# First weight blocks on a second DMA queue, and idle matmuls on a built-in constant

## The chip, the cores and the metric

The kernel runs on one core of one Trainium2 chip. The metric is the device time of one execution in microseconds: 135.92 us, the median of three runs (135.65 to 135.99). A core has five engines that run side by side, each with its own list of instructions: PE (TensorE, matrix products; its weight loads are listed as PEld), DVE (VectorE), ACT (ScalarE), POOL (GpSimd) and SP (SyncE, which here only issues DMAs). ACT and POOL can issue DMAs as well. An instruction that needs another engine's or a transfer's result waits on a semaphore, and everything behind it on its engine waits too.

## What is computed

Two branches over the same x of 2048 rows and 512 columns in bf16, mixed by a gate:

```
g = sigmoid((x * gate_w).sum(-1))
a = irfft2(rfft2(x) * (w_r + 1j * w_i))            # 2048 x 257 spectrum
h = x @ w1 + b1;  act = h * tanh(softplus(h));  b = act @ w2    # F = 1792
out = g * a + (1 - g) * b
```

The branch b is two dense layers with a Mish activation between them; the branch a is a Fourier filter, done as matrix products with small constant matrices and two exchanges through DRAM.

## The kernel before, in words

x is handled as 16 tiles of 128 rows, in 4 chunks of 4 tiles; w1's 1792 columns as 14 blocks of 128 (ft), and its 512 rows as 4 parts of 128 (dt). For a chunk, each x tile is transposed on PE (L516) with a permutation matrix as the weights, evicted from PSUM by DVE or ACT (L529 for the first chunk, L446 and L447 after), and then multiplied with the blocks of w1 (layer 1, L575); ACT applies Mish with the bias b1 while it evicts (L560). The second layer is L903. The steps of the filter branch (L609 to L612, L630, L745, L798, L828, L846) lie between them, and the layers fill PE where the filter branch waits.

The order of each engine's instructions is not written by hand. Every piece of work is a task with an engine, a planned duration, what it reads and writes, and a priority. `schedule` (L215) goes through the ready tasks, takes the one that can begin first by its own estimates (of those within 0.1 us the one with the highest priority), and so fixes a list for each engine. DMAs have a planned transfer time from their bytes and a rate `bw`; in the kernel before, all transfers of SP and ACT are planned as one line, one behind another (`dq_free`, L236 and L288 to L291). DMAs of one engine are issued in the order of the source. A planned duration affects only the order that is built, not the work.

The head is written apart. x's first chunk comes in two loads, `ld_x0(0)` for tiles 0 and 2 and `ld_x0(1)` for tiles 1 and 3 (L464). w1's first four blocks come in four loads, one for each of the 4 row parts (`ld_w1d`, L467), 128 KB each in rows of 1024 bytes. SP issues, in this order: x0(0), w1d0, x0(1), w1d1, w1d2, w1d3, w1's blocks 4 to 8 (512 KB), FD (a constant of the filter branch), x's second chunk (512 KB), w1's blocks 8 to 14, and the rest. ACT issues b1 alone (L474); POOL waits for w1's last load before it issues its own loads of w_r, w_i and w2. As soon as a pair of tiles and a row part of w1 are there, PE multiplies them: `early` for tiles 0 and 2, one row part at a time, `late` for tiles 1 and 3, one block at a time (both L590). b1 is transposed by a small product (L519) and evicted by ACT (`ev_small`, L521).

Until x arrives PE runs idle matmuls (`warm`, L502 to L505), whose results nobody reads. Their operand is a tile of zeros, `zt`, which DVE sets first (L500); they have 128 columns of weights and stream 256 columns. They are fillers: the planner puts one in wherever nothing better can begin on PE, and drops the rest when the first `early` task is planned (L239 to L243, L597). 14 of them are in the profile. The "table" task (L501) is an activation on one column, there so that ACT loads its function table early; it reads `zt` as well.

Of the kernel before, what the change touches and what calls it, by code (L numbers as in the profile page):

```python
# [7 lines left out]
BF = mybir.dt.bfloat16  # L8
F32 = mybir.dt.float32
AF = mybir.ActivationFunctionType  # L10
# [156 lines left out]
class _Graph:  # L167
# [47 lines left out]
    def schedule(self):  # L215
        tasks = self.tasks
        for t in tasks:
            t.succ = []
            t.start = -1.0
        for t in tasks:  # L220
            for d in t.deps:
                d.succ.append(t)
        for t in reversed(tasks):
            m = 0.0
            for s_ in t.succ:
                if s_.bl > m:
                    m = s_.bl
            t.bl = t.dur + t.lat + m
        nleft = {id(t): len(t.deps) for t in tasks}
        ready = [t for t in tasks if not t.deps]  # L230
        free = {e: 0.0 for e in self.ENGS}
        order = {e: [] for e in self.ENGS}
        nsched = 0
        EPS = SCH['eps']
        SYNC_LAT = SCH['sync']
        dq_free = 0.0  # L236
        dq2_free = 0.0
        while nsched < len(tasks):
            if self.filled is not None and self.filled.start >= 0:  # L239
                nsched += sum(t.filler for t in ready)  # L240
                ready = [t for t in ready if not t.filler]
                self.filled = None
                continue  # L243
            first = {}
            for t in ready:
                if t.isdma and t.idx < first.get(t.eng, 1 << 30):
                    first[t.eng] = t.idx
            best = None
            best_est = None
            ests = []  # L250
            for t in ready:
                if t.isdma and t.idx != first[t.eng]:
                    continue
                if t.opts is None:
                    est = free[t.eng]
                    for d in t.deps:
                        dd = d.done + SYNC_LAT + t.slack if d.eng != t.eng else d.start + d.dur if d.eng == "pe" else d.done
                        if dd > est:
                            est = dd
                else:  # L260
                    bo = None
                    for (oe, od, of) in t.opts:
                        e_ = free[oe]
                        for d in t.deps:
                            dd = d.done + (0.0 if d.eng == oe else SYNC_LAT)
                            if dd > e_:
                                e_ = dd
                        sc = e_ + od + (OPT_BIAS.get(oe, 0.0) if (self.win_first is not None and self.win_first.start >= 0 and self.win_last.start < 0) else 0.0)
                        if bo is None or sc < bo[0] - 1e-9:
                            bo = (sc, e_, oe, od, of)  # L270
                    est = bo[1]
                    t.eng, t.dur, t.fn = bo[2], bo[3], bo[4]
                ests.append((est, t))
                if best_est is None or est < best_est:
                    best_est = est
            best = None
            for est, t in ests:
                if est <= best_est + EPS:
                    if best is None:
                        best = (est, t)  # L280
                    elif (t.prio, t.bl, -t.idx) > (best[1].prio, best[1].bl, -best[1].idx):
                        best = (est, t)
            est, t = best
            ready.remove(t)
            t.start = est
            free[t.eng] = est + t.dur
            if t.isdma:
                if t.eng in ("sp", "act"):  # L288
                    xs = max(est + t.dur + 1.0, dq_free)
                    dq_free = xs + t.xfer  # L290
                    t.done = dq_free + 0.6 + 0.4 * (est > 12.0)  # L291
                else:
                    xs = max(est + t.dur + 1.2, dq2_free)
                    dq2_free = xs + t.xfer * 1.5
                    t.done = dq2_free + 1.0
            else:
                t.done = est + t.dur + t.lat + LAT[t.eng]
            order[t.eng].append(t)
            nsched += 1
            for s_ in t.succ:  # L300
                nleft[id(s_)] -= 1
                if nleft[id(s_)] == 0:
                    ready.append(s_)
        self.order = order
        self.makespan = max(t.done for t in tasks)
        return order
# [9 lines left out]
def _build(nc, A_x, A_w_r, A_w_i, B_x, B_w1, B_b1, B_w2, gate_w, out):  # L316
    cs = _build_consts()
    d_FD = nc.inline_tensor(_bf16_bits(cs["FD"]), name="c_fd").bitcast(BF)
# [7 lines left out]
    G = _Graph()  # L326
    es = ExitStack()
    with es:
        def sb(name, shape, dt):
            return es.enter_context(nc.sbuf_tensor(name, shape, dt))  # L330

        xo = sb("xo", [128, NT, 512], BF)
# [4 lines left out]
        act = sb("act", [128, 3, NFT, 512], BF)  # L337
        w1_sb = sb("w1_sb", [128, 4, F], BF)
        w2_sb = sb("w2_sb", [128, NFT, 512], BF)
        FDs = sb("FDs", [128, 768], BF)  # L340
# [6 lines left out]
        Ybuf = sb("Ybuf", [128, 32 * KR], BF)  # L347
        junk = sb("junk", [128, 512], BF)
        gwb = sb("gwb", [128, 512], BF)
        zt = sb("zt", [128, 256], BF)  # L350
        braw = sb("braw", [14, 128], BF)
        b1f = sb("b1f", [128, NFT], F32)
        gdot = sb("gdot", [128, NT], F32)
# [10 lines left out]
        xs = sb("xs", [128, 2, 2, 16], F32)  # L364
        rs = sb("rs", [128, 2, 16], F32)
        q1 = sb("q1", [128, 2, 2, 16], F32)
# [25 lines left out]
        ps = es.enter_context(nc.psum_tensor("ps", [128, 8, 512], F32))  # L392
        psb = ps.bitcast(BF)

        xv = A_x[0].rearrange("(s p b) d -> p s b d", s=2, b=8)
# [16 lines left out]
        def dma(name, dst, src, reads=(), writes=(), nbytes=0, deps=(), is_out=False, prio=None, queue="sp", bw=300e3):  # L412
            dur = 1.0 if queue == "pool" else 0.5

            def fn(e, _dst=dst, _src=src):
                return e.dma_start(_dst, _src)

            t = G.add(name, queue, dur, fn, reads=reads, writes=writes, lat=2.0 + nbytes / bw, deps=deps, prio=prio)
            t.xfer = nbytes / bw
            t.isdma = True  # L420
            if is_out:
                t.sem = out_sem
                n_out_dma[0] += 1
                t.semval = 16 * n_out_dma[0]
            else:
                t.sem = new_sem("d_" + name)
                t.semval = 16
            return t
# [30 lines left out]

        def ld_x(c, s0, s1):  # L460
            dma(f"ld_x{c}{s0}", xo[:, 4 * c + 2 * s0:4 * c + 2 * s1, :].rearrange("p (s b) d -> p s b d", b=2), xv[:, s0:s1, 2 * c:2 * c + 2, :],
                writes=[("x", t) for t in range(4 * c + 2 * s0, 4 * c + 2 * s1)], nbytes=128 * 2048 * (s1 - s0), bw=330e3 if c == 1 else 380e3)

        def ld_x0(b):  # L464
            dma(f"ld_x0{b}", xo[:, b:4:2, :], xv[:, :, b, :], writes=[("x", b), ("x", 2 + b)], nbytes=128 * 2048, bw=(218e3, 350e3)[b])

        def ld_w1d(dt_):  # L467
            dma(f"ld_w1d{dt_}", w1_sb[:, dt_, 0:512], w1v[:, dt_, 0:512], writes=[("w1d", dt_)], nbytes=128 * 1024, bw=350e3)

        def ld_w1(lo, hi):  # L470
            return dma(f"ld_w1_{lo}", w1_sb[:, :, 128 * lo:128 * hi], w1v[:, :, 128 * lo:128 * hi],
                       writes=[("w1", f) for f in range(lo, hi)], nbytes=512 * 256 * (hi - lo), bw=220e3 if lo == 4 else 380e3)

        dma("ld_b1", braw[:, :], B_b1.rearrange("(ft p) -> ft p", p=128), writes=["braw"], nbytes=3584, queue="act", prio=100.0)  # L474
        ld_x0(0)
# [1 line left out]
        ld_x0(1)  # L477
        for dt_ in range(1, 4):
            ld_w1d(dt_)
        ld_w1(4, 8)  # L480
        dma("ld_fd", FDs[:], d_FD[:], writes=["FD"], nbytes=128 * 1536, bw=262e3)
        ld_x(1, 0, 2)
        t_w1 = ld_w1(8, 14)
        dma("ld_m1", m1g1[:, 0:2048], d_M1.rearrange("p b h c m -> p (b h c m)"), writes=["m1"], nbytes=128 * 4096)
# [12 lines left out]
                writes=[("w2", h)], nbytes=128 * 7 * 1024, queue="pool", deps=[t_w1])  # L497


        G.add("zero", "dve", 0.15, lambda e: e.memset(zt[:, :], 0.0), writes=["zt"], prio=99.0)  # L500
        G.add("table", "act", 1.5, lambda e: e.activation(q1[:, 0, 0, 0:1], zt[:, 0:1], AF.Mish), reads=["zt"], prio=99.0)  # L501
        for i in range(NWARM):  # L502
            n_ = 256 if i < 15 else 128
            G.add(f"warm{i}", "pe", n_ / 1200, lambda e, n_=n_: e.matmul(ps[:, 6, 0:n_], zt[:, 0:128], zt[:, 0:n_], start=True, stop=True),  # L504
               reads=["zt"], prio=1.0).filler = True  # L505


        SP0 = PR['sp0']
        s1_tasks = []
        t_r1w = []  # L510
        def f_tr(e, ts, dts, at):
# [6 lines left out]

        pe("tr_small", 0.1, lambda e: e.transpose(psb[:, 0, 0:14], braw[0:14, :], id14[:, :]),  # L519
           reads=["braw", "id14"], writes=[("bank", 0)], prio=SP0 + 4.0)  # L520
        G.add("ev_small", "act", 0.25, lambda e: e.activation(b1f[:, :], psb[:, 0, 0:14], AF.Copy), reads=[("bank", 0)], writes=["b1f"], prio=SP0 + 1.05)  # L521
        for b in range(2):
            for dt_ in range(4):
                bk = (dt_ + 1) % 4
# [507 lines left out]
```

## Time and profile before

| | |
|---|---|
| median of three runs | 135.92 us (135.65 to 135.99) |
| the profiled execution: its time | 135.63 us |
| its span, first to last instruction | 133.9 us |
| PE, DVE, ACT, POOL busy | 96%, 66%, 59%, 20% |
| PE's share of the chain that ended last | 90% |
| loads: issue and time to landing | x0(0) 0.80 + 2.7; w1d0 1.31 + 3.4; x0(1) 1.81 + 3.6; w1 4 to 8 3.74 + 5.8; x's second chunk 4.76 + 7.0 us |

Times in the profile are from the first instruction, in us; a row of the timeline has the start, the length, the engine, the line, the operation with what it writes and reads, and how many instructions are merged in it. A matmul's own duration, from its start to its modelled end, is longer than the distance to the next one, since they are pipelined; the distance tells the rate. In a table by stage, each row has the stage, its length, PE's busy time and instructions, the clock that PE was granted, the busy share of the 16 DMA engines and GB/s.

### The profile page before, as it was taken

Reading aid. Unit: us, or ns where it says so; the run is one execution under the profiler, and the core shown is the slowest. Engines: PE = TensorE matmul, PEld = TensorE weight load, DVE = VectorE, ACT = ScalarE, POOL = GpSimd, SP = SyncE. Lnnn points to the kernel's source line nnn. Section 1 sums busy time; section 2 is a strip of 40 time slices with the busy share of each in tenths; the row PEclk is TensorE's granted clock in tenths of the full one; section 3 lists DMA queues with packets and bytes.
Section 4 is the critical chain, followed back from the end, with each engine's and each line's share of the span. In section 5 each row is a group of like instructions: output and inputs, shape, how many; then the busy total and the mean of one; then the engine's idle time right before and its main releaser. Section 6 shows DMA issues by size and latency. Waiting matters only on the chain.

```text
span 133.9 us, 2695 instructions
## 1 busy us (share of the span) xinstructions
PE 128.9 (96%) x1030; PEld 69.5 (52%) x1047; DVE 88.9 (66%) x213; ACT 79.6 (59%) x130; POOL 27.4 (20%) x56
## 2 busy tenths in 40 slices
PE   6999999999999999999999999999999999999992
PEld 4885655655544443443443443443445877755452
DVE  0286298989689982963893893794001699999422
ACT  4258798899988786605256657434333789792000
POOL 2000793014000009583440440440000000000000
PEclk9999999999999999999999999999999999999999
DMA  3899999999262399450600600600649700305321
GB/s 114 238 294 367 397 284 299 288 366 344 62 157 58 99 293 334 98 220 0 157 5 0 157 2 0 156 6 0 157 150 277 204 2 0 130 32 215 113 102 42
DMA packets 18937, 20.82 MB, mean 155 GB/s; under 512 B 1196, under 2 KB 16172, under 8 KB 18540
## 3 DMA queue, kind: packets, MB, share of 16 engines
q1 hardware_dynamic: 17888, 16.67, 41.1%
q0 software_dynamic: 864, 3.94, 9.4%
q8 instruction: 8, 0.13, 0.4%
q10 hardware_dynamic: 172, 0.04, 0.1%
q14 instruction: 5, 0.04, 0.1%
HBM read 14.35 MB, written 6.29 MB: 154 GB/s over the span
## 4 chain that ended last, share of the span: by engine, by line
PE 90%; ACT 6%; issue 1%; DVE 0%
PE ps L903 34%; PE ps L575 31%; PE ps L846 5%; ACT act L560 3%; PE ps L828 3%; ACT Ybuf L447 3%; PE ps L504 2%; PE ps L516 2%; PE ps L886 2%; PE ps L612 2%; PE ps L590 2%; PE ps L798 2%; PE ps L745 2%; PE ps L630 1%; PE ps L609 1%
## 5 line engine op out<-in xcount | busy, mean ns | idle before, releaser
L575 PE MATMUL ps<-xT,w_sb 128*128 128x512 bf16 x199 | 48.1, 379 | 0.8 <-issue 0.2
L903 PE MATMUL ps<-w_sb,act 128*128 128x512 bf16 x202 | 46.9, 379 | 0.6 <-issue 0.3
L560 ACT ACTIVATE act<-ps,b1f 128x512 bf16<-128x512 f32 x56 | 37.8, 692 | 12.8 <-PE ps L575 10.9
L903 PEld LDWEIGHTS ps<-w_sb,act 128*128 128x128 bf16 x210 | 20.2, 98 | 23.2 <-issue 1.2
L575 PEld LDWEIGHTS ps<-xT,w_sb 128*128 128x128 bf16 x208 | 19.4, 98 | 22.3 <-issue 2.1
L756 DVE TENSOR_TENSOR misc<-ps,WT 128x512 f32<-128x512 f32 x32 | 19.8, 681 | 5.9 <-PE ps L745 5.9
L858 ACT ACTIVATE xo<-ps,omg 128x512 bf16<-128x512 f32 x12 | 8.3, 690 | 19.5 <-PE ps L903 18.9
L762 POOL TENSOR_TENSOR misc<-misc 128x255 bf16<-128x255 f32 x17 | 12.1, 732 | 18.4 <-DVE misc L756 18.4
L446 DVE CAST Ybuf<-ps 128x512 bf16<-128x512 f32 (+1 forms) x9 | 8.2, 926 | 9.1 <-PE ps L798 7.3
L850 ACT ACTIVATE misc<-ps,gcol 128x512 f32<-128x512 f32 x16 | 10.7, 692 | 2.5 <-PE ps L846 2.4
L853 DVE TENSOR_TENSOR Tg<-misc 128x256 bf16<-128x256 f32 x32 | 11.7, 419 | 0.6 <-ACT misc L850 0.5
L446 DVE CAST misc<-ps 128x512 bf16<-128x512 f32 x7 | 4.8, 687 | 10.5 <-PE ps L828 10.5
L447 ACT ACTIVATE Ybuf<-ps 128x512 bf16<-128x512 f32 (+1 forms) x15 | 9.9, 714 | 2.9 <-PE ps L798 2.8
L649 DVE SCALAR_TENSOR_TENSOR junk<-xo,gwb 128x512 bf16<-128x512 bf16 x16 | 11.0, 690 | 0.7
L846 PE MATMUL ps<-GDs,misc 128*128 128x256 bf16 x64 | 9.3, 273 | 0.0
L447 ACT ACTIVATE Abuf<-ps 128x512 bf16<-128x512 f32 x13 | 7.7, 604 | 0.0
L446 DVE COPY xT<-ps 128x512 bf16<-128x512 bf16 x10 | 4.2, 422 | 4.6 <-PE ps L516 4.5
L516 PEld LDWEIGHTS ps<-pid,xo 128*128 128x128 bf16 x64 | 5.6, 111 | 3.1 <-DVE xT L446 0.4
L846 PEld LDWEIGHTS ps<-GDs,misc 128*128 128x128 bf16 x64 | 6.0, 98 | 2.1
L516 PE MATMUL ps<-pid,xo 128*128 128x128 bf16 x64 | 6.8, 243 | 0.0
L781 POOL TENSOR_TENSOR gexp<-gbase,gdot 128x16 f32<-128x16 f32 x1 | 2.9, 2943 | 18.5 <-DVE junk L649 18.5
L612 PE MATMUL ps<-FDs,Tg 128*128 128x256 bf16 x32 | 6.0, 273 | 0.0
(85 smaller groups left out, 112.8 us busy)
## 6 DMA issues: line engine op xcount, KB each, us to landing
scr<-Ybuf SPq DMA_DIRECT2D x16, 256.0 KB, 3.9
Abuf<-scr SPq DMA_DIRECT2D x4, 512.0 KB, 5.8
Abuf<-scr SPq DMA_DIRECT2D x8, 256.0 KB, 4.9
w_sb<-in_B_w_dram POOLq DMA_DIRECT2D x2, 896.0 KB, 14.2
out_dram<-xo SPq DMA_DIRECT2D x7, 256.0 KB, 2.1
xo<-in_A_x_dram SPq DMA_DIRECT2D x3, 512.0 KB, 9.8
WT<-in_A_w_r_dram POOLq DMA_DIRECT2D x4, 257.0 KB, 9.1
WT<-in_A_w_i_dram POOLq DMA_DIRECT2D x4, 257.0 KB, 10.8
```

The costliest lines, as they stand in the source:

```text
L446: G.add_multi(name, [("dve", dve_dur(n, rate=rate), lambda e: e.tensor_copy(out=dst, in_=src)), ("act", act_dur(n), lambda e: e.activation ...
L447: ("act", act_dur(n), lambda e: e.activation(dst, src, AF.Copy))],
L516: ins = e.transpose(psb[:, bank, 128 * col:128 * col + 128], xo[:, t, 128 * dt_:128 * (dt_ + 1)], perm[:, :])
L560: lambda e: e.activation(act[:, c % 3, ft, :].rearrange("p (t a b) -> p t a b", t=4, b=4), ps[:, bank, :].rearrange("p (t b a) -> p t a b" ...
L575: ins = e.matmul(ps[:, bank, :], w1_sb[:, dt_, 128 * ft:128 * (ft + 1)], xT[:, dt_, 4 * c:4 * c + 4, :], start=(dt_ == 0), stop=(dt_ == 3))
L649: lambda e, t=t: e.scalar_tensor_tensor(out=junk[:, :], in0=xo[:, t, :], scalar=1.0, in1=gwb[:, :], op0=ALU.mult, op1=ALU.mult, accum_out= ...
L756: lambda e, Pb=Pb, Wu=Wu, h=h, uu=uu, pb=pb: e.tensor_tensor(out=Pb[:, pb, :].rearrange("p (c j m) -> p c j m", c=2, j=2), in0=ps[:, 2 * h ...
L762: fz = (lambda e, c=c, Pb=Pb, op=op, pb=pb, h=h, uu=uu, zb=zb: e.tensor_tensor(out=Zb[:, zb, h, c, uu, 1:256], in0=Pb[:, pb, 1:256], in1=P ...
L846: ins = e.matmul(ps[:, yk, 256 * (j // 2):256 * (j // 2) + 256], TT[:, ts_, j // 2, s1, j % 2, :], GDs[:, j, :], start=(j % 2 == 0), stop= ...
L850: G.add(f"geo_{t}", "act", act_dur(512, True), lambda e: e.activation(gEO[:, gb, :], ps[:, yk, :], AF.Copy, scale=gcol[:, t:t + 1]), reads ...
L853: fg = (lambda e, i=i, op=op: e.tensor_tensor(out=ga[:, t, 256 * i:256 * i + 256], in0=gEO[:, gb, 0:256], in1=gEO[:, gb, 256:512], op=op))
L903: ins = e.matmul(ps[:, bank, :], act[:, hb, ft, 128 * tl:128 * (tl + 1)], w2_sb[:, ft, :], start=(ft == 0), stop=(ft == NFT - 1))
```

## The change

It has four parts. The loads `ld_w1d` of w1's first four blocks are issued by ACT, two ahead of the table task and two behind it by their priorities, and the planner keeps a line of its own for each of the two issuers. On SP the load of blocks 4 to 8 is split into 4 to 6 ahead of FD and 6 to 8 behind it, so that its rows have 512 bytes. The idle matmuls and the table task read a built-in constant of 1.0 that the start-up code sets on every core before any engine begins (it is a float32 column, read with a step of zero), in place of `zt`, which goes together with its memset; the idle matmuls have 32 columns of weights and stream 128 columns (the first eight) or 64. The eviction of the transposed b1 goes from ACT to DVE. Besides, planned rates and durations are changed, on which the order depends.

```diff
-        dq_free = 0.0
+        dq_free = {"sp": 0.0, "act": 0.0}
...
-                    xs = max(est + t.dur + 1.0, dq_free)
-                    dq_free = xs + t.xfer
-                    t.done = dq_free + 0.6 + 0.4 * (est > 12.0)
+                    xs = max(est + t.dur + 1.0, dq_free[t.eng])
+                    dq_free[t.eng] = xs + t.xfer
+                    t.done = xs + t.xfer + 0.6 + 0.4 * (est > 12.0)
...
-        zt = sb("zt", [128, 256], BF)
...
-                writes=[("x", t) for t in range(4 * c + 2 * s0, 4 * c + 2 * s1)], nbytes=128 * 2048 * (s1 - s0), bw=330e3 if c == 1 else 380e3)
+                writes=[("x", t) for t in range(4 * c + 2 * s0, 4 * c + 2 * s1)], nbytes=128 * 2048 * (s1 - s0), bw=210e3 if c == 1 else 380e3)
...
-            dma(f"ld_x0{b}", xo[:, b:4:2, :], xv[:, :, b, :], writes=[("x", b), ("x", 2 + b)], nbytes=128 * 2048, bw=(218e3, 350e3)[b])
+            dma(f"ld_x0{b}", xo[:, b:4:2, :], xv[:, :, b, :], writes=[("x", b), ("x", 2 + b)], nbytes=128 * 2048, bw=(330e3, 200e3)[b])
...
-            dma(f"ld_w1d{dt_}", w1_sb[:, dt_, 0:512], w1v[:, dt_, 0:512], writes=[("w1d", dt_)], nbytes=128 * 1024, bw=350e3)
+            dma(f"ld_w1d{dt_}", w1_sb[:, dt_, 0:512], w1v[:, dt_, 0:512], writes=[("w1d", dt_)], nbytes=128 * 1024, bw=(125e3, 150e3, 262e3, 262e3)[dt_],
+                queue="act", prio=99.8 - 0.5 * (dt_ > 1))
...
-                       writes=[("w1", f) for f in range(lo, hi)], nbytes=512 * 256 * (hi - lo), bw=220e3 if lo == 4 else 380e3)
+                       writes=[("w1", f) for f in range(lo, hi)], nbytes=512 * 256 * (hi - lo), bw={4: 160e3, 6: 291e3}.get(lo, 380e3))
...
-        ld_w1(4, 8)
-        dma("ld_fd", FDs[:], d_FD[:], writes=["FD"], nbytes=128 * 1536, bw=262e3)
+        ld_w1(4, 6)
+        dma("ld_fd", FDs[:], d_FD[:], writes=["FD"], nbytes=128 * 1536, bw=200e3)
+        ld_w1(6, 8)
...
-        G.add("zero", "dve", 0.15, lambda e: e.memset(zt[:, :], 0.0), writes=["zt"], prio=99.0)
-        G.add("table", "act", 1.5, lambda e: e.activation(q1[:, 0, 0, 0:1], zt[:, 0:1], AF.Mish), reads=["zt"], prio=99.0)
+        ones = nc.const_aps.tensor(1.0, (128, 256))
+        G.add("table", "act", 1.5, lambda e: e.activation(q1[:, 0, 0, 0:1], ones[:, 0:1], AF.Mish), prio=99.5)
         for i in range(NWARM):
-            n_ = 256 if i < 15 else 128
-            G.add(f"warm{i}", "pe", n_ / 1200, lambda e, n_=n_: e.matmul(ps[:, 6, 0:n_], zt[:, 0:128], zt[:, 0:n_], start=True, stop=True),
-               reads=["zt"], prio=1.0).filler = True
+            n_ = 128 if i < 8 else 64
+            G.add(f"warm{i}", "pe", n_ / 600, lambda e, n_=n_: e.matmul(ps[0:32, 6, 0:n_], ones[:, 0:32], ones[:, 0:n_], start=True, stop=True),
+                  prio=1.0).filler = True
...
-        G.add("ev_small", "act", 0.25, lambda e: e.activation(b1f[:, :], psb[:, 0, 0:14], AF.Copy), reads=[("bank", 0)], writes=["b1f"], prio=SP0 + 1.05)
+        G.add("ev_small", "dve", 0.15, lambda e: e.tensor_copy(out=b1f[:, :], in_=psb[:, 0, 0:14]), reads=[("bank", 0)], writes=["b1f"], prio=SP0 + 1.05)
...

```

## The prediction

> **What bounds the kernel now.** I read the page's busy times, then PE's own waits, then the table by stage, then PE's timeline of the head and the landings of the first loads.
>
> ```profile
> PE 128.9 (96%) x1030; PEld 69.5 (52%) x1047; DVE 88.9 (66%) x213; ACT 79.6 (59%) x130; POOL 27.4 (20%) x56
> ...
> PE 90%; ACT 6%; issue 1%; DVE 0%
> ...
> PE ps L504 <- DVE zt L500: 1.1, 1, 1.1
> PE ps L903 <- issue: 0.3, 2, 0.2
> PE ps L575 <- issue: 0.2, 1, 0.2
> PE ps L575 <- ACT act L560: 0.2, 1, 0.2
> ...
> 1.11:4.31 3.20, 3.19 (x16) 1.00 0.65 202
> 4.31:7.20 2.89, 2.89 (x23) 1.00 0.86 234
> 7.20:10.10 2.90, 2.90 (x28) 1.00 0.92 297
> 10.10:40.00 29.90, 29.25 (x322) 1.00 0.91 286
> ...
> 1.11 2.10 PE L504 MATMUL ps<-zt 128*128 128x256 bf16 x9 [1.11 <-DVE zt L500]
> 3.15 0.19 PE L519 MATMUL ps<-pid,braw 14*128 14x14 bf16 x1
> 3.27 1.25 PE L504 MATMUL ps<-zt 128*128 128x256 bf16 x5
> 4.31 1.06 PE L516 MATMUL ps<-pid,xo 128*128 128x128 bf16 x8
> 5.16 1.06 PE L590 MATMUL ps<-xT,w_sb 128*128 128x256 bf16 x4
> 6.01 1.06 PE L516 MATMUL ps<-pid,xo 128*128 128x128 bf16 x8
> 6.87 3.40 PE L590 MATMUL ps<-xT,w_sb 128*128 128x256 bf16 x28
> ...
> L590 PE MATMUL ps<-xT,w_sb x6: 344/421/421, 5.2 to 7.1; 128*128 128x256 bf16 x6
> ...
> L590 PE MATMUL ps<-xT,w_sb x28: 272/273/421, 6.9 to 10.0; 128*128 128x256 bf16 x28
> ```
>
> PE is the bound from 4.31 us on: after its first instruction it waits for nothing longer than 0.2 us, and between 10.1 and 131.5 us it idles only about 1.5 us. A shift of the head is therefore passed on to the end almost whole, and nothing later than the head is touched by the diff except through the planner's order.
>
> In the head two things count. First, PE runs at half rate until about 7.1 us: four L590 matmuls take 6.01 - 5.16 = 0.85 us, 0.213 each for 256 columns, and their rows read 421 ns; later rows read 273 ns and some 27 fill the 2.90 us from 7.20 on, about 0.108 each. (The clock column says 1.00 in these first stages; the matmul rows contradict it.) Second, real work starts at 4.31 although the first x load, issued at 0.80, lands 2.7 us later, at 3.50. The gap is five more idle matmuls of L504, planned ahead and not to be interrupted.
>
> **The change, part by part.**
>
> *Start of the idle matmuls.* They no longer wait for DVE's memset (0.17 us, begun at 0.89). SP and ACT leave the start barrier at 0.80; PE can too. They start 0.31 us earlier. The "table" activation loses the same wait, which its DMA issue (ACT is busy to 1.47) covered anyway.
>
> *How long they last.* The planner fills PE until the first transposes can go. Worked by hand with its changed entries, that is eight of 128 columns and ten of 64, some 1664 columns, against 14 of 256 before. What a column costs no row shows, for the constant is float32. The low end is the bf16 row: 0.213/256 = 0.83 ns, 1.39 us in all, and then x's landing binds. The high end is matmuls that do not overlap at all: the L516 rows at half clock are 314 ns for 128 columns, so some 260 for 64, and 8 x 0.314 + 10 x 0.26 = 5.1 us. I take twice the bf16 row, 2.77 us, since the element has four bytes instead of two; between the ends it is the nearer to neither, and the entry in the diff (columns/600) says the same. With 0.25 us around the small transpose (3.03 to 3.27 now), the idle block ends at 0.80 + 2.77 + 0.25 = 3.82. Weight loads (151 ns for 128 columns at half clock, here 32) lie under the matmuls; uncovered they would add at most 18 x 0.151 = 2.7 us, which lies inside the high end.
>
> *First x.* It is first on SP's queue as before and shares the DMA engines only from about 2.6 us (w1's first block, issued by ACT at 1.47, plus the 1.15 us that x needs from issue to first packet). It lands between 3.50 as now and, at half the rate for the last 70 KB, 3.8. With 0.2 us from weight load to matmul the transposes start between 3.8 and 4.05. I take 3.82: 0.49 us earlier than 4.31. This is work at half rate, worth 0.24 us at full rate.
>
> *The clock step.* It came 6.0 us after the first idle matmul. If it follows the start of activity it comes 0.31 us earlier, worth 0.155 us; if it stays where it was, nothing. [...]
>
> *w1 on ACT.* SP loses four issues of 0.45 us, and gains one for the split of block 4 to 8; x's fourth issue onward goes out 1.5 us sooner. ACT gains four issues: after b1 (0.80 to 1.47) two, to 2.4; then table load and activation (1.28 + 0.20), to 3.9; then two more, to 4.8. Its first eviction is due at about 4.6 instead of 4.98 and would wait up to 0.2 us; who waits is the second set of transposes, due at 5.5, so this is covered. If the sequencer issues past the table load they go out at 2.5 and nothing waits. w1's blocks landed at 4.7, 6.0, 6.4 and 7.5; used at 5.1, 6.8, 7.4, 7.8, now to be used about 0.4 us sooner. Their own queue does not have them behind x, so I cost them at nothing; the last has 0.3 us of slack today and would cost up to 0.1 us if it landed where it does now.
> [...]
>
> *Small things.* The eviction of b1 (0.18 us) moves from ACT to DVE, idle until 4.76: nothing. The memset saved: nothing further. POOL's loads still wait for w1's last load.
>
> *Sum.* 0.24 + 0.155 = 0.40 us less. Against the profiled execution that is 135.63 - 0.40 = 135.23; its span is 133.9 and 1.7 lie around it. The median of the runs shown is 135.92, 0.29 above, so 135.5. The planner's order after 10 us may change with its new rates; PE has 1.5 us of waits there in all, so I allow 0.4 us to either side.
>
> **Rivals.**
>
> *The idle matmuls run long (slower).* One mechanism: float32 columns at four bf16 columns each, 1664 x 3.33 ns = 5.55 us, ending at 6.60. The transposes then start 2.3 us late, 1.15 us of full-rate work lost, less 0.155 for the clock: 136.9; without the clock's help 137.1; without overlap (5.1 us) 136.7. It decides from about 2.6 bf16 columns on, where the block ends at 4.62 and the clock's gain is spent. For it: the constant's memset row is float32. Against it: the rate of a matmul row here follows its columns, and nothing in this trace shows an operand read four times. If the unbroken block brought the clock early, the loss would shrink to some 0.4 us.
> [...]
>
> [...]
>
> [...]
>
> *The loads are the bound (no gain).* x's next part (issued at 4.76, landing 7.0 us later at 11.8) is used at 11.94 and has as many bytes ahead of it as before. Landing at the same 11.8 it takes away all but 0.1 us; split w1 rows of 512 instead of 1024 bytes could make it 0.3 us later: 135.8 to 136.2. Against it: x's issue is 1.5 us sooner, and the DMA engines have 14 to 35% free before 7.2 us.
>
> **How the numbers follow.** Of a change within 0.3% (0.41 us) a measurement of this kernel can tell little. Forecast 0.38 (faster 0.23, same 0.13, slower 0.02, since 0.40 sits at the bound); long idle matmuls 0.25 (slower 0.20, same 0.02, faster 0.03); early clock 0.12, faster; late clock 0.08, slower; loads 0.17 (faster 0.04, same 0.07, slower 0.06). Together faster 0.42, same 0.22, slower 0.36. The predicted time is the forecast's, 135.5, whose own range is 135.1 to 135.9. Both signs hold much of the chance, so the range goes from the early clock's 134.7 to the long idle matmuls' 137.0; left out are the late clock and the far end of the four-column case.
>
> **What would show it.** L504's rows (now reading the constant) should start at 0.8 and end near 3.8, at some 0.21 and 0.11 us each; L516 should start near 3.8 to 4.05; the 421 ns rows should end near 6.8; the last L590 should start near 9.6 instead of 10.0; and PE's waits should list no load. The prediction is wrong if L504 still runs after 4.6, if L516 or L590 waits for a DMA, if half-rate rows go on past 7.2, or if PE's idle time after 10 us grows by more than the gain.

## The result and the profile after

The changed kernel takes 137.05 us (median of six runs, 136.72 to 137.43); the kernel before, run beside it on the same chip, takes 135.67 us (six runs, 135.49 to 135.99). The ratio is 1.010, with a 95% interval of 1.0078 to 1.0122: about 1% slower. The ratios in this document leave out executions that lie more than 1.5% above the fastest of their kernel, while the medians count all. The profiled execution took 137.0 us with a span of 135.3 us, 1.4 us more than the span of before. In the changed kernel's file the line numbers of the head are higher by one: the idle matmuls are L505, the transposes L517, `early` and `late` L591, layer 1 L576.

The page of the changed kernel, busy times and shares of the chain that ended last:

```profile
PE 131.7 (97%) x1069; PEld 70.5 (52%) x1069; DVE 88.7 (66%) x213; ACT 79.1 (58%) x129; POOL 26.8 (20%) x56
...
PE 89%; DMA 4%; ACT 3%; ACTq 1%; issue 0%; DVE 0%
```

PE is still the bound, but a DMA now has 4% of the chain; before, none was in it. PE's waits (us in all, times, longest):

```profile
PE ps L505 <- PEq L1018: 0.8, 1, 0.8
PE ps L591 <- DMA w_sb<-in_B_w_dram: 0.2, 1, 0.2
```

The memset's wait is gone, and a wait for w1 is new. PE's timeline of the head (start, length, operation, number of instructions):

```profile
0.83 4.45 PE L505 MATMUL ps<-const-float32-1.0 128*32 128x128 f32 x24 [0.83 <-PEq L1018]
5.21 0.18 PE L520 MATMUL ps<-pid,braw 14*128 14x14 bf16 x1
5.32 0.88 PE L505 MATMUL ps<-const-float32-1.0 128*32 128x64 f32 x12
6.13 0.62 PE L517 MATMUL ps<-pid,xo 128*128 128x128 bf16 x8
6.80 0.61 PE L591 MATMUL ps<-xT,w_sb 128*128 128x256 bf16 x4
7.25 0.61 PE L517 MATMUL ps<-pid,xo 128*128 128x128 bf16 x8
8.03 3.64 PE L591 MATMUL ps<-xT,w_sb 128*128 128x256 bf16 x28 [0.17 <-DMA w_sb<-in_B_w_dram]
```

The first transposes start at 6.13 us, where they started at 4.31. The idle matmuls run until then, although x's first load landed at 3.55 as before. The last row of L591 starts at 11.39 us; in the kernel before the last one started at 9.99. PE's end moves by 1.43 us (131.45 to 132.88). So 1.40 of it is made in the head, and the rest of the program adds next to nothing.

The waits hide partly in the modelled ends of the matmuls. They are plainer by tile: for the instructions that read w1 (`w_sb`), up to 12 us, what they waited for, and which of them waited for its loads (us, times):

```profile
  DMA w_sb<-in_B_w_dram: 1.1, 4
...
  PEld ps L591: 1.0, 3
  PE ps L591: 0.2, 1
```

Three weight loads wait as well: the four row parts of w1's first four blocks land at 5.38, 7.98, 8.62 and 9.26 us, where they landed at 4.69, 5.99, 6.36 and 7.52. The table by stage (stage, length and busy time of PE, clock, DMA share, GB/s) shows that this is not for want of traffic:

```profile
1.11:4.31 3.20, 3.20 (x17) 1.00 0.59 176
4.31:7.20 2.89, 2.84 (x34) 1.00 1.01 316
7.20:10.10 2.90, 2.67 (x26) 1.00 1.08 378
```

The DMA engines move 316 and 378 GB/s in the two last stages; before it was 234 and 297. More is moved, but other things than the blocks PE waits for.

**Where the 1.40 us come from.** In two experiments below the load waits are absent (e2, e9) and the same float32 idle matmuls run; from the first transpose to the last row of L590/L591 the head then takes 4.51 us in both (6.49 to 11.01, and 6.56 to 11.08), all at full rate. With this the changed kernel would have come to 6.13 + 4.51 = 10.64, which is 0.65 later than before: the late start of real work (1.82 us) less what the earlier full rate saves (5.68 - 4.51 = 1.17). The remaining 11.39 - 10.64 = 0.75 us are waits for w1. These two shares hold for the profiled executions. The step to full rate came at 6.13 and 6.28 us in e2 and e9, and between 5.0 and 5.3 here, although PE runs the same instructions until then; in e2, with its later step, the head ends 1.02 us later than before (11.01 against 9.99) without any wait for w1.

### The profile page after: what moved, and what is told of

It is laid out like the page before. It is cut to its first block, busy times and chain, and to the rows that moved or that the text cites. A ratio compares the mean times of both kernels' runs of the same rounds, so it can differ in the third digit from the quotient of the medians.

```text
span 135.3 us, 2759 instructions
## 1 busy us (share of the span) xinstructions
PE 131.7 (97%) x1069; PEld 70.5 (52%) x1069; DVE 88.7 (66%) x213; ACT 79.1 (58%) x129; POOL 26.8 (20%) x56
## 4 chain that ended last, share of the span: by engine, by line
PE 89%; DMA 4%; ACT 3%; ACTq 1%; issue 0%; DVE 0%
PE ps L904 34%; PE ps L576 33%; PE ps L847 5%; DMA w_sb<-in_B_w_dram 4%; PE ps L591 3%; PE ps L829 3%; PE ps L887 2%; PE ps L613 2%; PE ps L799 2%; PE ps L746 2%; PE ps L517 1%; PE ps L631 1%; ACT Ybuf L446 1%; ACT act L561 1%; PE ps L610 1%; ACTq L415 1%
## 5 line engine op out<-in xcount | busy, mean ns | idle before, releaser
L576 PE MATMUL ps<-xT,w_sb 128*128 128x512 bf16 x208 | 49.6, 380 | 0.1
L904 PE MATMUL ps<-w_sb,act 128*128 128x512 bf16 x210 | 48.3, 380 | 0.0
L576 PEld LDWEIGHTS ps<-xT,w_sb 128*128 128x128 bf16 x208 | 19.3, 98 | 22.3 <-issue 1.9
L517 PEld LDWEIGHTS ps<-pid,xo 128*128 128x128 bf16 x64 | 4.6, 98 | 3.0 <-DVE xT L445 0.5
L505 PE MATMUL ps<-const-float32-1.0 128*32 128x64 f32 (+1 forms) x36 | 5.3, 330 | 0.8 <-PEq L1018 0.8
## 6 DMA issues: line engine op xcount, KB each, us to landing
WT<-in_A_w_i_dram POOLq DMA_DIRECT2D x4, 257.0 KB, 11.6
```

Source lines behind the costliest of these rows:

```text
L576: ins = e.matmul(ps[:, bank, :], w1_sb[:, dt_, 128 * ft:128 * (ft + 1)], xT[:, dt_, 4 * c:4 * c + 4, :], start=(dt_ == 0), stop=(dt_ == 3))
L904: ins = e.matmul(ps[:, bank, :], act[:, hb, ft, 128 * tl:128 * (tl + 1)], w2_sb[:, ft, :], start=(ft == 0), stop=(ft == NFT - 1))
```

## The experiments

All sums of the output are computed as in the reference in every kernel here; e8 leaves out only idle matmuls, whose results nobody reads. Two causes are in question: the idle matmuls (theory I) and the loads (theory L). Ratios are to the kernel before, run beside each batch (135.6 to 135.8 us).

### One part at a time: e1 and e2

e1 keeps the new loads and makes the idle matmuls cheap again, by a bf16 constant, with the columns doubled so that the planned order stays:

```diff
+        onesb = nc.const_aps.tensor(1.0, (128, 256), BF)
...
-            n_ = 128 if i < 8 else 64
-            G.add(f"warm{i}", "pe", n_ / 600, ... ones[:, 0:32], ones[:, 0:n_] ...
+            n_ = 256 if i < 8 else 128
+            G.add(f"warm{i}", "pe", n_ / 1200, ... onesb[:, 0:32], onesb[:, 0:n_] ...
```

> The changed kernel with its idle matmuls on the bf16 constant, 256 and 128 columns in place of 128 and 64 in float32; their planned time is the same, and so is the order of everything else. In the changed kernel the idle block ran from 0.83 to 6.13 us and the last L591 was over at 11.5, against 10.1 before. Theory I, the idle matmuls cost the time: the block ends near 3.9, the transposes start at 3.9 to 4.1 and the time falls to 135.4 to 135.9. Theory L, w1's blocks land late on ACT's queue (the last at 9.3 against 7.5): the transposes start at 3.9 as well, PE then waits for w1 until about 9.3, and the time stays at 136.8 to 137.2.

e2 keeps the float32 idle matmuls and puts the loads back on SP's queue, unsplit:

```diff
-            dma(f"ld_w1d{dt_}", ..., bw=(125e3, 150e3, 262e3, 262e3)[dt_], queue="act", prio=99.8 - 0.5 * (dt_ > 1))
+            dma(f"ld_w1d{dt_}", ..., bw=350e3)
...
-        ld_w1(4, 6)
+        ld_w1(4, 8)
         dma("ld_fd", ...)
-        ld_w1(6, 8)
```

> The changed kernel with its loads as before (w1's first four blocks on SP's queue, blocks 4 to 8 unsplit, the old planned rates except x's first), but with the float32 idle matmuls, 18 as in the changed kernel. Theory I: the block ends near 6.1, the last L590-type matmul is over at about 10.75, and the time is 136.2 to 137.0. Theory L: w1's blocks land by 7.5 as before, no wait for them, and the time falls to 135.5 to 135.9 although the idle block is as long. If both hold together, each hides behind the other: e1 near 137.0 and this one near 136.3.

e1 measured 136.79 us, ratio 1.0079 (1.0058 to 1.0100); e2 136.35 us, ratio 1.0057 (1.0038 to 1.0076). Each part is a loss by itself, 1.2 and 0.8 us, and together they cost 1.4, not 2.0: presumably because w1's late blocks cost less while PE is late from idle matmuls. e1's timeline and waits show the loads without the cover:

```profile
PE ps L592 <- DMA w_sb<-in_B_w_dram: 1.2, 3, 0.7
```

```profile
3.93 1.03 PE L518 MATMUL ps<-pid,xo 128*128 128x128 bf16 x8
5.28 1.01 PE L592 MATMUL ps<-xT,w_sb 128*128 128x256 bf16 x4 [0.31 <-DMA w_sb<-in_B_w_dram]
6.08 0.95 PE L518 MATMUL ps<-pid,xo 128*128 128x128 bf16 x8
7.71 1.22 PE L592 MATMUL ps<-xT,w_sb 128*128 128x256 bf16 x8 [0.68 <-DMA w_sb<-in_B_w_dram]
9.13 2.36 PE L592 MATMUL ps<-xT,w_sb 128*128 128x256 bf16 x20 [0.20 <-DMA w_sb<-in_B_w_dram]
```

The real work starts at 3.93, 0.38 earlier than before, and all of that and more is lost in three waits for w1. In e2 the transposes start at 6.49 and no load is waited for:

```profile
6.49 0.62 PE L515 MATMUL ps<-pid,xo 128*128 128x128 bf16 x8
7.17 0.61 PE L589 MATMUL ps<-xT,w_sb 128*128 128x256 bf16 x4
7.61 0.61 PE L515 MATMUL ps<-pid,xo 128*128 128x128 bf16 x8
8.06 3.22 PE L589 MATMUL ps<-xT,w_sb 128*128 128x256 bf16 x28
```

Theory I and theory L are both right.

**What a float32 column costs.** The groups by shape, up to 7 us, of the changed kernel:

```profile
L505 PE MATMUL ps<-const-float32-1.0 128*32 128x128 f32 x16 | 3.6, 420 | 0.8 <-PEq L1018 0.8
L505 PE MATMUL ps<-const-float32-1.0 128*32 128x64 f32 x20 | 1.9, 258 | 0.0
```

Eight matmuls of 128 columns and ten of 64 were written, and there are 16 and 20 instructions: each float32 matmul is executed as two. At half rate the starts of the wide ones lie 0.213 us apart, those of the narrow ones 0.107, so each instruction takes 0.213/128 = 1.67 ns a column, and each written column 3.33 ns. A bf16 column takes 0.213/256 = 0.83 ns at that rate, also in e1's idle matmuls. Float32 is four times bf16 here, 3.33 against 0.83 ns, and the rows show it as two instructions, each at twice the time of a bf16 column.

### Why the moved loads are late: e3, e5, e6, e11

With four loads taken off it, SP issues the rest of w1, FD and x's second half megabyte 1.4 to 2 us sooner, beside ACT's four. Theory S: these later loads take the DMA engines from w1's first blocks. The DMA queues of the changed kernel between 5.4 and 8.0 us (packets, MB, share of 16 engines' time), q1 being SP's and q10 ACT's (before, q10 carried only b1's 28 packets by 16 us; the change adds 0.53 MB to it):

```profile
DMA packets 1232, 0.91 MB, mean 350 GB/s; under 512 B 82, under 2 KB 1211, under 8 KB 1232
...
q1 hardware_dynamic: 883, 0.60, 72.9%
q10 hardware_dynamic: 349, 0.31, 35.5%
```

ACT's queue, on which PE waits, gets a third: 0.31 of 0.91 MB, 119 GB/s. SP's alone had 257 GB/s in the same stretch of the kernel before. e3 and e5 hold SP's later loads back, e3 until the second row part of w1 has landed, e5 until x0(0) has:

```diff
 e3 (e1 and:)
-        ld_w1(4, 6)
+        ld_w1(4, 6, deps=[w1d1's load])
 e5 (e1 and:)
-        ld_x0(0)
+        t_x0 = ld_x0(0)
...
-        ld_w1(4, 6)
+        ld_w1(4, 6, deps=[t_x0])
```

> The kernel of e1, but SP waits for the landing of w1's second row part before it issues blocks 4 to 6 and all that follows; ACT's queue then has only x beside it. Theory S, ACT's blocks are late because SP's later loads share the DMA engines with them: the second row part lands near 5.0 to 5.5 instead of 8.0 and the last near 6.5 to 7.2 instead of 9.3. Theory Q, four loads of 128 KB on ACT's queue are slow by themselves: they land at 7.5 and at 9.0 or later even so. The time says less, since blocks 4 to 8 and x's second chunk come about 2 us later than in e1: 135.8 to 137.2.

> The kernel of e1 (bf16 idle matmuls, w1's first row parts on ACT's queue), but SP waits for the landing of x's first load, near 3.6 us, before it issues blocks 4 to 6 and what follows. This is a smaller dose than in e3 of the same cure: ACT's queue has a lead of some 2 us before SP's later loads come beside it. Theory S (shared DMA engines): the last row part lands between e3's 6.4 and e1's 9.1, near 7.5, x's second chunk between 11.5 and 12.5, and the time is 135.6 to 136.4, between the kernel before and e1. If the cure takes from x's second chunk as much as it gives to w1, the time stays at 136.3 or more as in e3.

In e3 the row parts land at 5.12, 5.85, 6.07 and 6.39 us, in place of 5.14, 7.67, 8.28 and 9.09 in e1. Only SP's later issues differ, so theory S is shown. The last row of L591 starts at 9.09, but the time is 136.32, ratio 1.0058 (1.0028 to 1.0088), since SP's issues now start at 5.86, and x's second chunk lands at 13.91:

```profile
PE ps L591 <- DMA w_sb<-in_B_w_dram: 0.7, 1, 0.7
PE ps L517 <- DMA xo<-in_A_x_dram: 0.4, 1, 0.4
```

e5 holds SP back only to 3.6 us. w1 lands at 5.29, 5.72, 5.96 and 6.28, x's second chunk at 11.6, and the time is 135.21, ratio 0.9968 (0.9956 to 0.9980): the first kernel here that is faster than before, if its two long executions are left out (more on them below). Its queues between 3.6 and 5.0 us:

```profile
q10 hardware_dynamic: 379, 0.35, 79.6%
q1 hardware_dynamic: 89, 0.08, 17.5%
```

With nothing new behind x on SP's queue, ACT's gets 0.35 of 0.43 MB.

Is the split of blocks 4 to 8 to blame, with its small rows? e11 is e1 with the load in one piece again, on SP and ahead of FD; only the split is undone:

```diff
-        ld_w1(4, 6)
+        ld_w1(4, 8)
         dma("ld_fd", ...)
-        ld_w1(6, 8)
```

> The kernel of e1 with blocks 4 to 8 in one load ahead of FD, in rows of 1024 bytes in place of 512: the split is undone, all else of the moved loads stays. If rows of 512 bytes or the split are what pushes w1's first blocks back on ACT's queue, these land at 8 or earlier and the time falls to 136.0 to 136.4. If any backlog on SP does it, they land at 8.7 to 9.5 and the time stays at 136.5 to 137.2.

e11 measured 137.73, ratio 1.0143 (1.0117 to 1.0169), with w1 at 5.83, 7.31, 8.87 and 10.02. The split is not the cause: with the unsplit load, all of whose bytes go out a microsecond sooner, the blocks land later still. e6 turns the queues round: x, w1's first blocks and x's second chunk on SP as before, and blocks 4 to 8 and FD on ACT's, held until x0(0) has landed:

```diff
-        ld_w1(4, 6)
-        dma("ld_fd", ..., bw=200e3)
-        ld_w1(6, 8)
+        ld_w1(4, 8, deps=[t_x0], queue="act", prio=98.9)
+        dma("ld_fd", ..., bw=262e3, queue="act", prio=98.8)
```

> The roles exchanged: x and w1's first row parts in one line on SP as in the kernel before, x's second chunk right behind them, and the later w1 blocks 4 to 8 and FD on ACT's queue, issued when x's first load has landed; bf16 idle matmuls of e1. If both queues together move more than one (378 against 297 GB/s from 7.2 to 10.1 us in the changed kernel and before), and what is first on SP keeps its landing, then w1's row parts land by 7.5, x's second chunk near 10.5 in place of 11.8 to 12.1, no wait for loads is longer than 0.3 us, and the time is 135.0 to 135.5. If blocks 4 to 8 beside them push w1's row parts back, as the moved loads did, these land at 8 or later and the time is 135.9 to 136.6.

It was much worse than expected: 139.11 us, ratio 1.0224 (1.0190 to 1.0258), with single executions from 137.89 to 142.34. The profiled one is the longest of them. In it blocks 4 to 8, issued on ACT at 3.80, landed at 13.22, and PE waited:

```profile
PE ps L575 <- DMA w_sb<-in_B_w_dram: 4.1, 1, 4.1
```

After that wait PE was at half rate again for some 6 us (granted clock 0.5 from 12.2 to 19.0): four L575 in 1.9 us, elsewhere 1.03. So in these kernels it is ACT's queue that comes off worse beside a backlog on SP, with the urgent loads on it or the later ones: 0.31 MB to SP's 0.60 in the changed kernel (5.4 to 8.0 us), 0.28 to 0.46 in e1 (5.4 to 7.6), 0.25 to 0.68 in e11 (5.4 to 8.0) and 0.49 to 0.83 in e6 (5.5 to 10.0). By what rule the two queues share the DMA engines the packets do not settle: in the changed kernel there are 349 of ACT's to 883 of SP's while both queues had work, but in e6 there are 477 to 518, nearly one for one. Why ACT gets less stays open.

A second thing makes the blocks late. The profile has 16 updates for each of these loads, and the load counts as landed with the last. In the changed kernel w1's second row part had 8 of 16 updates at 6.09, 15 at 6.52 and the last at 7.98; the third 15 at 7.77 and the last at 8.62. So in the second part the last update alone came 1.5 us behind the others. In the kernel before the same part had 8 at 5.07, 15 at 5.92 and the last at 5.99. In e12, which repeats e5, they came at 5.30, 5.74 and 5.94. That fits a tail that grows with the backlog, but it wasn't tested alone, and the kernel before has longer tails in later loads (21.73 and 24.13 us for GD's last two updates). Its cause stays open.

### What the idle matmuls are worth: e4, e8, e9

e9 is the changed kernel with e5's hold: the float32 idle matmuls, no load trouble.

```diff
-        ld_w1(4, 6)
+        ld_w1(4, 6, deps=[t_x0])
```

> The changed kernel as it is, float32 idle matmuls and all, with the one addition of e5: SP waits for x's first load before it issues blocks 4 to 6 and what follows. The loads of w1 are then out of the way (last part near 6.3), and only the idle matmuls are left: 18 float32 ones until about 6.1 us at a clock step near 5. If they alone cost what lies between e5 (135.21) and the changed kernel (137.05) once the loads are cured, the time is 135.8 to 136.4: transposes at 6.1, the last L591 near 10.7, no wait for w1. If the moved loads were the whole loss, 135.1 to 135.4.

136.35 us, ratio 1.0049 (1.0029 to 1.0068), no wait for w1, the transposes at 6.56. Against the same loads with bf16 idle matmuls in the same batch (e12, 135.53) the float32 ones cost 0.8 us.

e4 is the other useful half of the idea without the loads: the kernel before, its idle matmuls unchanged in size but reading a bf16 constant, so that nothing waits for the memset. x0's planned rate is raised too, so that one idle matmul fewer is planned:

```diff
-        zt = sb("zt", [128, 256], BF)
...
+        ones = nc.const_aps.tensor(1.0, (128, 256), BF)
...
-            ... zt[:, 0:128], zt[:, 0:n_] ..., reads=["zt"]
+            ... ones[:, 0:128], ones[:, 0:n_] ...
```

> The kernel before, all loads in its order on SP, with only two things of the change: idle matmuls (128 columns of weights, bf16 as before) read the built-in constant and so start 0.3 us earlier, and x's first load is planned at the rate 330, so that 13 of them are planned instead of 14. This is the forecast's gain without the moved loads: transposes at 3.8 instead of 4.3, time 135.2 to 135.5. If w1's loads bind as soon as PE starts earlier, or the clock step does not move, 135.5 to 135.8.

135.91 us, ratio 1.0019 (0.9997 to 1.0041): nothing gained. The transposes start at 4.31 as before and not at 3.8: in the profiled execution PE waits 0.45 us for b1, and x's first load lands only at 4.18. The step to full rate comes near 6.2 us in place of 7.2, and so the last row of L589 starts at 9.51, 0.48 earlier than before. PE's timeline shows where that went:

```profile
12.13 0.40 PE L515 MATMUL ps<-pid,xo 128*128 128x128 bf16 x4 [0.29 <-DMA xo<-in_A_x_dram]
```

x's second chunk landed at 12.08 in this execution. The transposes that read it started at 12.16 in the kernel before and at 12.13 here, and PE's work ends at 131.38, 0.07 earlier. In e3 and e4 the gain of the head meets this load next. e7 therefore puts that load ahead of FD and of blocks 6 to 8 in e4:

```diff
-        ld_w1(4, 8)
-        dma("ld_fd", ...)
+        ld_w1(4, 6)
         ld_x(1, 0, 2)
+        dma("ld_fd", ...)
+        ld_w1(6, 8)
```

> The kernel of e4 (before, with bf16 idle matmuls from the built-in constant, all loads on SP), with x's second chunk issued ahead of FD and of w1's blocks 6 to 8, and planned accordingly. In e4 PE finished the last L589 0.48 us earlier than before, and waited 0.29 us for this chunk, which landed at 12.08. If that landing is what took the gain, it lands near 10.3 here and the time is 135.0 to 135.4, below the kernel before. If the gain went elsewhere, or FD and blocks 6 to 8 are now waited for as long, 135.5 to 136.0.

135.82 us, ratio 1.0022 (1.0001 to 1.0043). x's chunk landed at 11.33, a microsecond later than expected, and PE waited for other loads instead, 0.3 us for FD and 0.5 for w1, although full rate came at 4.25 us. This swap on one queue only moved the wait. e8 has no idle matmuls at all:

```diff
-NWARM = 60
+NWARM = 0
```

> The kernel before without any idle matmul. PE's first work is then the small transpose near 2.8 us and the transposes near 3.7. What the idle matmuls are worth: if full rate follows PE's activity by 3 to 6 us (steps seen: 3.7 to 7.2 us after the span's start, with activity from 0.8 or 1.1), it comes at 7 to 10 us, up to 3 us later than before, and up to 1.5 us are lost less 0.25 for the earlier start: 135.6 to 137.0. If it does not depend on them, 135.2 to 135.5.

136.00 us, ratio 1.0033 (1.0013 to 1.0052): the last row of the head starts at 10.13, and full rate comes at 7.9 us instead of 7.2. All idle matmuls of the kernel before together are worth about 0.4 us, about half of what the float32 ones cost in place of bf16 (0.8).

### Whether the moved loads can be worth something: e10, e12 to e15

e5's gain of 0.3% is near what can be measured, and two of its twelve executions took 137.1 us, among them the profiled one. e12 runs the same kernel again; e10 puts the first row part of w1 back on SP (with planned rates to match), so that PE is not held up for it:

```diff
-                queue="act", prio=99.8 - 0.5 * (dt_ > 1))
+                queue="act" if dt_ else "sp", prio=99.8 - 0.5 * (dt_ > 1))
```

> The kernel of e5 once more, unchanged, on the same chip as e9 to e11: it gave 135.21, ratio 0.9968 with an interval below 1. If that holds it is faster than both kernels again, 134.9 to 135.5, with w1's last row part near 6.3 and x's second chunk near 11.6; an execution in which full rate comes only near 9.8 us, as in the profile of e5, takes about 137.

> The kernel of e5 with w1's first row part back on SP between x's two first loads; the other three stay on ACT's queue. In e5 the first row part landed at 5.29 and PE waited 0.5 us for it at 4.9. Here it should land near 4.6 as in the kernel before, the first L592 at 4.8, and the time falls by 0.1 to 0.4 us below e5's, to 134.9 to 135.2. If the second half of x or the other parts come later by as much, or x's second chunk binds as in e4, the time stays at 135.1 to 135.5.

e12: 135.53 us, ratio 0.9982 (0.9955 to 1.0009), three of twelve executions at 136.9 to 137.3. e10: 135.45 us, 0.9999 (0.9971 to 1.0028), two of twelve at 136.9 and 137.0; its first part of w1 lands 0.6 us sooner and x's second chunk 0.7 later. The long executions can be told in the profiles of e5 and e12, whose kernels are the same. e5, in the long one:

```profile
6.23 1.06 PE L518 MATMUL ps<-pid,xo 128*128 128x128 bf16 x8
7.08 4.53 PE L592 MATMUL ps<-xT,w_sb 128*128 128x256 bf16 x28
```

e12, in an ordinary one:

```profile
6.05 0.61 PE L518 MATMUL ps<-pid,xo 128*128 128x128 bf16 x8
6.50 3.22 PE L592 MATMUL ps<-xT,w_sb 128*128 128x256 bf16 x28
```

Full rate comes at 9.8 us in the first and at 6.0 in the second: a late step of the clock, in an execution that is 1.5 to 2 us longer. PE waits 0.46 and 0.34 us for w1's first part there, between the first transposes and the first `early`. Two theories: the gap keeps the clock low (theory gap), or the idle matmuls' 32 columns do (theory columns). e13 fills the gap with four idle matmuls that depend on the transposes, and should have no execution near 137 under theory gap; e14 gives the idle matmuls 128 columns of weights.

```diff
 e13 (e5 and:)
+        for i in range(4):
+            G.add(f"gap{i}", "pe", 0.0, ... onesb[:, 0:32], onesb[:, 0:128] ..., deps=[last of the first transposes])
 e14 (e5 and:)
-            ... e.matmul(ps[0:32, 6, 0:n_], onesb[:, 0:32], onesb[:, 0:n_], ...)
+            ... e.matmul(ps[:, 6, 0:n_], onesb[:, 0:128], onesb[:, 0:n_], ...)
```

> The kernel is e5 (bf16 idle matmuls, first four blocks of w1 on ACT's queue, SP's later loads held back until x's first half chunk has landed) with four more idle matmuls of 128 columns between the first transposes and the first early matmul. [...] If the 32 weight columns are the cause (theory columns): one to three executions of the set stay near 137, the rest at 134.9 to 135.5. [...]

> The kernel is e5 with idle matmuls whose weights have 128 columns in place of 32. Theory columns: none of the executions near 137, median 135.1 to 135.5, and the step to full rate not later than 6.1 us in the profile. Theory gap: as e5 and e12, one to three executions near 137 and the rest at 134.9 to 135.6, ratio 0.996 to 0.999. The first early matmul waits for the first block of w1 until 5.1 to 5.3 us under both.

> The kernel of e13 once more, on another chip. Theory gap: again no execution of twelve over 136.5, median 135.0 to 135.6, ratio 0.995 to 1.000. Theory that e13 was luck: two to four of twelve at 136.7 to 137.3, as in e5, e12, e10 and e14.

e14: 135.25 us, 0.9969 (0.9939 to 0.9999), but four of twelve at 136.7 to 137.3, so 128 columns of weights do not prevent it. e13: 135.51 us, 0.9983 (0.9962 to 1.0005), none over 136.1. e15, the same kernel: 135.37 us, 0.9975 (0.9953 to 0.9996), one of twelve at 137.4. e13's timeline:

```profile
3.93 0.83 PE L519 MATMUL ps<-pid,xo 128*128 128x128 bf16 x8
4.69 0.40 PE L537 MATMUL ps<-const-bfloat16-1.0 128*32 128x128 bf16 x4
5.21 0.60 PE L598 MATMUL ps<-xT,w_sb 128*128 128x256 bf16 x4
```

The hole is filled, and full rate is there at 4.4 us. Together: 9 late executions of 36 with the gap (e5, e12, e14), 1 of 24 with it filled (e13, e15). Were they equally likely, so uneven a split would come about once in 25 times. But e10 has no such gap in its profile, and two late executions of twelve:

```profile
4.01 1.03 PE L518 MATMUL ps<-pid,xo 128*128 128x128 bf16 x8
4.84 1.06 PE L592 MATMUL ps<-xT,w_sb 128*128 128x256 bf16 x4
```

With e10 there are 3 of 36 without the gap, and chance would make so uneven a split about once in nine times. So the gap is a suspect; that it is the cause is not shown. The filled kernel is some 0.2% faster than before, with one interval just below 1 and one that just includes it. With all executions counted its means are 135.40 and 135.53 us (before: 135.70 and 135.75), while those of e5, e12 and e14 are 135.50, 135.76 and 135.77 (before: 135.61, 135.72 and 135.70). More than that can't be said. In e13's profile x's second chunk lands at 11.62 and its transposes start at 12.12, hardly sooner than before, and yet PE's work ends 0.70 us earlier (130.75): a gain of the head can get past this load.

## Why the prediction was wrong, point by point

It foretold 135.5 us and no wait for a load; 137.05 came, with a wait. Both main steps failed, and the range failed with them: its upper end, 137.0, took in the long idle matmuls alone.

- **"I take twice the bf16 row, 2.77 us."** This step failed. The price is four times the row, 3.33 ns a written column at half rate. The block with its small transpose ran from 0.83 to 6.03 us, against a forecast end of 3.82. The 18 idle matmuls and their columns were counted right. The rival of long idle matmuls named the price and 6.60 as the end; the block was shorter because its last rows ran at full rate. That this rival's 136.9 lies close to the measured 137.05 is luck: it holds no wait for a load, and those made more than half of the loss in the head (0.75 of 1.40). What misled me was to take a value between two far ends and to find support for it in the planned duration (columns/600): a planned duration is what somebody believed, not a row. That "nothing in this trace shows an operand read four times" was no argument, since no float32 matmul was in the trace at all.
- **"Their own queue does not have them behind x, so I cost them at nothing."** This failed as well, and by itself would have made the change a loss: e1 measures it at 1.2 us. Their own queue did not keep them clear of what SP sends. What I listed on the side of the gain, that x's fourth issue and all behind it go out 1.5 us sooner, is the cause: SP's backlog took two thirds of what was moved (0.60 of 0.91 MB), and with SP held back in e3 the parts landed 1.8 to 2.7 us sooner, all but the first. The spare 14 to 35% of the engines that I saw was used indeed (350 against 257 GB/s), but mostly not by these loads. A want of bandwidth is not what did the harm: more was moved here, and it was shared out badly.
- **The clock step, "0.31 us earlier".** Wrong in size, on the good side. The last rows at half rate start at 4.97 and the next ones, from 5.32, are at full rate; before it came at about 7.2. That is 1.9 us earlier, and but for the small transpose only idle matmuls of 32 columns had run: 32 columns of weights did not keep full rate away here. This is why 1.82 us of late start cost only 0.65, between the rival's "some 0.4 us" and its 1.15. How much of the 1.9 us is owed to the change is open, and luck has a part in it: kernels that run the same PE instructions up to 3.9 us had the step at 3.8 (e3, by its rows), 4.4 (e13), 6.0 (e12), 6.8 (e1) and 9.8 us (e5), with one profile each.
- **The rival of loads as the bound** named the right load for the next obstacle. In the changed kernel x's second chunk lands at 11.04, sooner than before, and is not waited for; but in e3 and e4, where the head is early, PE waits 0.4 and 0.3 us for it. That rows of 512 bytes would make it 0.3 us later was my estimate, and no run shows it. In e4 0.48 us of gain in the head left 0.07 at PE's end, so on the old order of loads the forecast of 0.40 us less would have been cut to little.
- **The chances of an early and of a late clock**, 0.12 and 0.08, and the range's lower end of 134.7 take the step to come sooner or later by a fixed amount, which no run shows; the profiles have it anywhere from 3.8 to 9.8 us. In e7's profile full rate comes at 4.25 and the last row of the head at 9.45, held up by loads. It brought no gain there (135.82), since loads were waited for. e13's profile has the step at 4.40, the last row of the head at 9.10 and a time of 134.90, near that lower end.
- **Right:** the start at 0.8 (0.83); x's first landing (3.55, forecast 3.50 to 3.8); ACT's issues past the table load (2.44 to 3.33, while the table loads from 2.37 to 3.65), so that its first eviction isn't late; b1's eviction on DVE at no cost; and that what is lost in the head is passed on whole (1.40 there, 1.43 at PE's end), with the planner's order worth 0.03 of the 0.4 us allowed.

## What to carry to other kernels

Price an operation of a type that the trace does not show by its worst sensible row, or measure it, before it goes on the path: here a built-in constant saved 0.3 us of waiting and its float32 type cost 0.8. When loads are moved to another issuer, ask what the old issuer will send in the time that it gains; that goes to the same DMA engines, and here the urgent loads got only a third of what was moved (0.31 of 0.91 MB) until the other queue was held back. And where a head becomes shorter, look for the next load by its landing time first: in e4 half a microsecond gained ended at a load that landed no sooner than before.

## What the runs showed of the hardware

- A float32 matmul is two instructions, each at two bf16 columns' time: 1.67 ns a column and instruction at half rate, and 58 ns for 64 columns at full rate.
- Beside SP's backlog ACT's queue had 0.31 of 0.91 MB between 5.4 and 8.0 us, and in e6 it needed 9.4 us for 512 KB.
- The two queues together moved 350 GB/s between 5.4 and 8.0 us, where SP's alone moved 257 in the kernel before. That it takes a second queue for this is not shown: from 11.2 to 14.2 us of the kernel before, with other loads, SP's queue alone moved more, as this row of the DMA view has it:

```profile
DMA packets 601, 1.22 MB, mean 408 GB/s; under 512 B 30, under 2 KB 398, under 8 KB 601
```

- The last of a load's 16 updates came long after the fifteenth in these: 1.5 us for w1's second row part in the changed kernel, 2.4 us for GD in the kernel before.
- ACT's sequencer issued two DMAs (2.44 to 3.33 us) during its table load (2.37 to 3.65).
- The step to full rate came between 3.8 us (e3) and 9.8 us (e5) after the first instruction, in kernels with the same PE instructions up to 3.9 us. In e6 PE's granted clock fell to 0.5 at 12.2 us, during a wait of 4.1 us, and stayed there to 19.0. What sets these times, no run here shows.
